# A layernorm, attention and GeGLU kernel on one core: score maxima, fills and splits moved in the prologue and first FFN sections

## The chip, the core and the metric

The kernel runs on one core of a Trainium2 chip. A core has TensorE (matrix products into PSUM, with a separate path that loads weights), VectorE (DVE), ScalarE (ACT) and GpSimd (POOL), which read and write SBUF and PSUM, and SyncE (SP), whose queue here issues the transfers. Each engine works through its own list of instructions in order; one engine waits for another only where an instruction needs its result or its buffer. The metric is the device time of one execution in microseconds (us), taken as the median over runs.

## The reference

x has 2048 rows of 576. The layernorm of x feeds an attention with 32 heads of width 18 and a GeGLU network with 4608 hidden columns, and the two results are joined:

```python
xn = _layernorm(x)
qkv = (xn @ wqkv).reshape(B, S, 3, H, Dh).transpose(2, 0, 3, 1, 4)
q, k, v = qkv[0], qkv[1], qkv[2]
p = _softmax(einsum("bhqd,bhkd->bhqk", q, k) * Dh ** -0.5)
s = einsum("bhqk,bhkd->bhqd", p, v).transpose(0, 2, 1, 3).reshape(B, S, D) @ wo
g = _silu((_gelu(xn @ w_gate) * (xn @ w_up)) @ w_down)
out = x + s * g
```

All values are fp32.

## The kernel before

**Products in parts.** A matrix product is made from operands that are split into a high part, rounded to TensorE's fp32r format, and a low part, what the rounding left. Three products (high by high, high by low, low by high) add up in PSUM. So every weight tile and every activation needs a split ahead of its use: a copy that makes the high part and a subtraction that makes the low one. `split` (L117, L119) does both on GpSimd. `split_ap` (L123, L124) copies on ScalarE and subtracts on GpSimd, and `split_av` copies on ScalarE and subtracts on VectorE.

**Prologue.** Rows come in four blocks of 512. `norm` normalises a block (for block 0 partly on ScalarE), `transposes` turns it on TensorE into five pieces of 128 columns, and `split_t` splits these: the first four into `xth` and `xtl` (L204 for the high part), the last, of 64 columns, into `xtr` (L208). Then `project` multiplies nine weight tiles of 128 query or key columns, in the order (4, 5, 0, 1, 6, 7, 8, 2, 3), with 14 products of 128x512 each (L196); `po` is their sum in PSUM, in three buffers, and `qh` and `ql` are a tile's high and low parts. Weight tiles arrive in `rawp`. The columns that do not fill a tile are the "rest". Tile 4 is the first one and has its own code: its high part is made by ScalarE (`first_hi`), its low part by GpSimd (L355), both at fixed places in their engines' lists. Tiles 5, 0, 1 and so on go through `split_qk`, whose place in GpSimd's list the scheduler chooses. Queries, keys and values are stored to DRAM.

**FFN sections.** The gate and up products are made in sections, each of 27 pairs of 64-row products (L431: `pg` and `pu` are the sums, `xd` the activations, `wh` and `wl` the weights' parts) over 128 hidden columns for 512 rows. A section's pairs take its weights' three groups one after the other, and each group's low part `wl` comes behind its high part. While section n runs, the weights of section n+1 are split: two groups near its start, one at its end. Then `activate` computes the hidden values: a square on ScalarE, VectorE's products at L441 and L445, a tanh on ScalarE at L446, and VectorE's last product at L448. The hidden values are split into `ah` (L457) and `al` (L460).

**Down products.** After every two sections the hidden values meet w_down. `T` holds the two parts of a piece of w_down, which arrives in `rawd` (one buffer). For the first five parts, `down_plain` (L529) makes 48 products `py`, and VectorE adds the sums to `M` (L531). For these, `cut_plain_b` splits w_down: ScalarE copies 128x1152 (L457), GpSimd subtracts (L460), as a hook at pair 4 of the odd section. From the sixth part on, sums of pieces of w_down are made first, by GpSimd into `tsum` (`sums_b`, L494), in the section before they are used, and seven combined products take the place of eight (`down`, L542).

**The lead.** Attention's softmax needs each row's maximum before its exponentials. A score pair for the maxima (`max_pair`: products `pm` at L814, then VectorE's reduction at L815) is issued one unit ahead of the score pair that is used (`pe`, L861, then ScalarE's exponential at L862). So the maxima of the first unit and a quarter of the second, 32 + 8 = 40, must be made before the attention starts with section 11. They are spread over sections 0 to 10; `FIRST` (L41) says how many go into each, and `spread` sets them between the 27 pairs. `KA` and `QT` hold the keys and queries for these products; rows that no load fills are set once to a constant (L761, L764). When 32 maxima of unit 0 are issued, `max_parts(0)` follows: VectorE reduces them to negated maxima `nm` (L821), splits those (L825, L826) and transposes them (L831), SP stores the result and loads it into `QT`. The last three are hooks at numbered pairs of the next section.

**What sets the order.** TensorE's order is the program's. So is SP's from the attention's set-up on. VectorE, ScalarE and GpSimd are ordered by a scheduler, which keeps the items passed to `keep_in_program_order` in their order. The PSUM sums `pgu`, `pm`, `pe`, `acc` and `py` share a ring of three buffers, so a late reduction holds up TensorE's next product.

Of the kernel before, what the change touches and what calls it, by code (L numbers as in the profile page):

```python
# [20 lines left out]
NB = S // TB  # L21
# [19 lines left out]
FIRST = (0, 0, 3, 5, 3, 5, 3, 6, 4, 6, 5)  # L41
# [47 lines left out]
def kernel(ctx: ExitStack, tc: tile.TileContext, x, wqkv, wo, w_gate, w_up, w_down, out):  # L89
# [78 lines left out]

    TERMS = [(0, k, 0) for k in range(KT)] + [(1, k, 0) for k in range(KT)] + [(0, k, 1) for k in range(KT)] \
# [5 lines left out]
    with tc.tile_pool(name="pro", bufs=1) as pro, tc.tile_pool(name="pps", bufs=1, space=PSUM) as pps:  # L175
# [43 lines left out]
        def norm(xr, b, between=None, behind=None):  # L219
            keep = tc.keep_in_program_order if b == 1 else lambda i: i  # L220
            st = pro.tile([P, 4, 8], F32, name="st", bufs=2)
            for j in range(4):
                bs = pro.tile([P, 2, 6], F32, name="bs", bufs=2)
                for h in range(2):
                    one = nc.vector.bn_stats(bs[:, h, :], xr[j][:, 288 * h:288 * h + 288])
                    keep(one)
                if behind and j == 0:
                    behind(one)
                nc.vector.bn_aggr(st[:, j, 0:2], bs)
# [21 lines left out]
            if between:  # L251
                between()
# [95 lines left out]
        def first_hi():  # L348
            tc.keep_in_program_order(nc.scalar.activation(qhi, ahead_qk[0][1], AF.Copy))

        xr = load_x(0)
        last = norm(xr, 0, first_hi, first_loads)
        raw, (raw_r, rest) = ahead_qk.pop(0)[1], ahead_qk.pop(1)
        QR.extend(rest)
        lo = nc.gpsimd.tensor_tensor(qlo, raw, f(qhi), op=ALU.subtract)  # L355
        after(lo, last, "VectorE alone on the first x")
        tc.keep_in_program_order(lo)
        split(QR[0][:, c0], QR[1][:, c0], raw_r[:, c0], tc.keep_in_program_order)
# [4 lines left out]
        for b in range(NB):  # L363
            for n, t in enumerate(ORDER):
                if b == 0 and n == 1:
                    nc.sync.dma_start(zeros.rearrange("i x -> (i x)").rearrange("(p x) -> p x", p=P), zz)
                if n == (2 if b == 0 else 0) and b + 1 < NB:
                    xr = load_x(b + 1)
                if b == 0 and ahead_qk:
                    first = split_qk(*ahead_qk.pop(0))  # L370
                    if n < 3:
                        after(first, last, "VectorE alone on the first x")
                    if n + 4 < NQT:
                        ahead_qk.append(load_qk(ORDER[n + 4]))
                if b == 0 and n == 4:
                    raw_r, VR = load_rest(2 * D, D)
                    split_av(VR[0], VR[1], raw_r, tc.keep_in_program_order)
                if b == 0 and n in (5, 6):
                    raw_v.append(load_wv(n - 5))
                if b == 0 and n in (7, 8):  # L380
                    split_wv(n - 7, raw_v[n - 7])
                project(b, t, xt)
                if n == 4 and b + 1 < NB:
                    norm(xr, b + 1)
# [193 lines left out]
    def section(specials=(), tag="f", slots=False):  # L578
# [20 lines left out]
        if n == 0:  # L599
            load_rawd(0)  # L600
        if g == 0 and (b, r) in FORMED:
            raw = FF["rawd"]
            hook(12, lambda: sums_b(raw))
# [30 lines left out]
    def finish():  # L634
# [16 lines left out]
        if b == 0 and r < PLAIN:  # L651
            if g == 0:
# [101 lines left out]
    with tc.tile_pool(name="att", bufs=1, reuse_waits="tile") as att:  # L754
# [4 lines left out]
        for i, kk in enumerate(KS):  # L759
            for r in range(2):  # L760
                (nc.vector, nc.gpsimd)[i % 2].memset(f(kk[r]), 1.0)  # L761
        QT = [att.tile([P, 2, TB], F32R, name=f"QT{i}") for i in range(3)]
        for t in QT:
            nc.gpsimd.memset(f(t), 0.0)  # L764
# [52 lines left out]
        def max_neg(u):  # L817
# [6 lines left out]
            eng = nc.gpsimd if u > 0 else nc.vector  # L824
            keep(eng.tensor_copy(m2[:, :, 0], n2))  # L825
            keep(eng.tensor_tensor(m2[:, :, 1], n2, f(m2)[:, :, 0], op=SUB))  # L826
# [13 lines left out]
        def max_parts(u):  # L840
            max_neg(u)
            for i, part in ((8, max_turn), (9, max_store), (18, max_end)) if u > 0 else ((0, max_turn), (1, max_store), (14, max_end)):
# [373 lines left out]
```

## Time and profile before

| | |
|---|---|
| time, median of 3 runs | 2559.25 us (2558.43 to 2561.18) |
| profiled execution, its own time | 2558.65 us |
| its span in the trace | 2556.6 us |
| TensorE busy | 2540.1 us (99% of the span) |
| VectorE busy | 2089.0 us (82%) |
| GpSimd busy | 1644.7 us (64%) |
| ScalarE busy | 1462.6 us (57%) |
| mean clock granted to TensorE | 0.999 of full speed |

Rows that are quoted below come from different views of one trace. In the timeline of an engine a row is a start, a busy time, engine, line, operation, output<-inputs, shape, and xN for N instructions in a row; a bracket at its end is the time for which the engine had stood idle, and what ended that. In the list of groups an SPq row is SP's issue of a transfer. Chain rows give a start, a length, engine, name and line. A table of stretches gives a window, its length, and each engine's busy time with the number of instructions.

### The profile page before, as it was taken

What the parts mean: (1) busy time and instruction counts of PE and PEld (TensorE: products, weight loads), DVE (VectorE), ACT (ScalarE), POOL (GpSimd) and SP (SyncE); (2) the same over time, 40 slices, a digit from 0 to 9 for tenths busy, and PEclk for the clock granted to TensorE, in tenths of its full rate; (3) what the DMA queues carried; (4) which work ended last, traced back from release to release, by engine and by line L of the source; (5) the groups of instructions that cost most, each with busy time, mean ns of one, the idle gap of its engine ahead of it and who ended that gap; (6) DMA issues with size and microseconds to landing.
All of it is one profiled execution on the core that took longest, in us unless ns stands there. A gap on an engine that the chain in (4) does not pass through costs nothing.

```text
span 2556.6 us, 52908 instructions
## 1 busy us (share of the span) xinstructions
PE 2540.1 (99%) x20548; PEld 1840.8 (72%) x20548; DVE 2089.0 (82%) x2364; ACT 1462.6 (57%) x1765; POOL 1644.7 (64%) x1714
## 2 busy tenths in 40 slices
PE   9999999999999999999999999999999999999999
PEld 8888866676667766666666666766666776666788
DVE  5326888989888888888887889889898888888367
ACT  3224366666666665566666556555566665556631
POOL 3105588888888875666667566666667666666773
PEclk9999999999999999999999999999999999999999
DMA  8854455555585565677787677666668666665775
GB/s 259 273 187 134 106 165 160 167 168 158 162 220 162 167 172 142 163 169 169 169 194 192 162 169 168 174 168 157 160 159 213 164 173 172 163 167 153 190 212 209
DMA packets 410321, 446.88 MB, mean 175 GB/s; under 512 B 107092, under 2 KB 287060, under 8 KB 410072
## 3 DMA queue, kind: packets, MB, share of 16 engines
q1 hardware_dynamic: 410072, 443.50, 65.4%
q8 instruction: 164, 2.69, 0.5%
q14 instruction: 85, 0.70, 0.1%
HBM read 347.30 MB, written 96.08 MB: 173 GB/s over the span
## 4 chain that ended last, share of the span: by engine, by line
PE 97%; DVE 1%; POOL 1%; ACT 0%; DMA 0%; issue 0%; SPq 0%; POOLq 0%; DVEq 0%; ACTq 0%
PE pg L431 25%; PE acc L878 18%; PE py L542 15%; PE pm L814 9%; PE pe L861 9%; PE pu L431 9%; PE po L196 7%; PE po L1032 2%; PE pgu L431 1%; PE py L529 1%; DVE mx L815 0%; PE pt L268 0%; DMA rawp<-in_A_wqkv_dram 0%; POOL wl L124 0%; ACT pT L862 0%
## 5 line engine op out<-in xcount | busy, mean ns | idle before, releaser
L862 ACT ACTIVATE pT<-pe 128x1024 f32<-128x1024 f32 x1024 | 1048.1, 1027 | 572.7 <-PE pe L861 539.6
L815 DVE TENSOR_REDUCE mx<-pm 128x2 f32<-128x1024 f32 x1024 | 1220.2, 1224 | 166.5 <-PE pm L814 150.5
L431 PE MATMUL pu<-xd,wh 64*128 64x512 f32 x2466 | 902.2, 396 | 0.0
L431 PE MATMUL pg<-xd,wh 64*128 64x512 f32 x2466 | 901.3, 396 | 0.0
L431 PEld LDWEIGHTS pg<-xd,wh 64*128 64x128 f32 x2466 | 455.0, 185 | 114.4 <-issue 55.6
L431 PE MATMUL pg<-xd,wl 64*128 64x512 f32 x1233 | 481.4, 390 | 1.1 <-POOL wl L124 1.1
L431 PE MATMUL pu<-xd,wl 64*128 64x512 f32 x1233 | 481.6, 391 | 0.0
L431 PEld LDWEIGHTS pu<-xd,wh 64*128 64x128 f32 x2466 | 455.0, 184 | 17.5 <-ACT xd L160 0.2
L878 PE MATMUL acc<-pT,VS 128*32 128x512 f32 x4096 | 466.0, 595 | 0.0
L117 POOL TENSOR_SCALAR wh<-raw 128x384 fp32r<-128x384 f32 x402 | 218.7, 546 | 372.9 <-PE pu L431 262.0
L119 POOL TENSOR_TENSOR wl<-raw,wh 128x384 fp32r<-128x384 f32 x402 | 415.8, 1036 | 28.5
L814 PE MATMUL pm<-KA,QT 64*128 64x512 f32 x2048 | 413.7, 395 | 6.4 <-ACT pT L862 3.3
L861 PE MATMUL pe<-QT,KA 64*128 64x512 f32 x2048 | 411.0, 392 | 0.0
L542 PE MATMUL py<-T,ah 128*128 128x288 f32 x1876 | 380.6, 298 | 0.0
L549 DVE TENSOR_TENSOR M<-py,M 128x576 f32<-128x576 f32 x448 | 339.6, 758 | 31.7 <-PE py L542 18.1
L542 PEld LDWEIGHTS py<-T,ah 128*128 128x128 f32 x1876 | 298.4, 188 | 54.0 <-issue 54.0
L460 POOL TENSOR_TENSOR al<-h,ah 128x512 fp32r<-128x512 f32 (+1 forms) x143 | 295.6, 2067 | 61.5 <-ACT ah L457 51.7
L878 PEld LDWEIGHTS acc<-pT,VS 128*32 128x32 f32 x4096 | 120.1, 109 | 276.8 <-issue 229.7
L542 PE MATMUL py<-T,al 128*128 128x288 f32 x938 | 275.7, 294 | 0.0
L861 PEld LDWEIGHTS pe<-QT,KA 64*128 64x128 f32 x2048 | 192.9, 184 | 109.7 <-DVE mx L815 24.4
L431 PEld LDWEIGHTS pg<-xd,wl 64*128 64x128 f32 x1233 | 227.6, 185 | 36.4 <-POOL wl L124 2.0
L814 PEld LDWEIGHTS pm<-KA,QT 64*128 64x128 f32 x2048 | 198.9, 185 | 54.6 <-ACT pT L862 9.3
(174 smaller groups left out, 3001.7 us busy)
## 6 DMA issues: line engine op xcount, KB each, us to landing
T<-ts SPq DMA_DIRECT2D x98, 576.0 KB
KA<-qk SPq DMA_DIRECT2D x768, 72.0 KB
T<-ts SPq DMA_DIRECT2D x98, 432.0 KB
raw<-in_B_w_gate_dram SPq DMA_DIRECT2D x144, 288.0 KB
raw<-in_B_w_up_dram SPq DMA_DIRECT2D x144, 288.0 KB
ts<-T SPq DMA_DIRECT2D x36, 576.0 KB
VS<-vs SPq DMA_DIRECT2D x128, 152.0 KB
qk<-t SPq DMA_DIRECT2D x72, 256.0 KB
```

The source lines that it names most:

```text
L117: first = nc.gpsimd.tensor_scalar(hi, raw, 1.0, 1.0, op0=ALU.mult, op1=ALU.mult)
L119: keep(nc.gpsimd.tensor_tensor(lo, raw, f(hi), op=ALU.subtract))
L196: nc.tensor.matmul(o, st, m, start=(i == 0), stop=(i == len(terms) - 1))
L431: nc.tensor.matmul(o, w[1 + wp][k][rr, c, :], xd[k][xp][rr, c, :], start=(i == 0), stop=(i == len(terms) - 1))
L460: keep(two.tensor_tensor(lo, raw, f(hi), op=ALU.subtract))
L542: nc.tensor.matmul(py[:, t, 0:DC], h[:, i, tt], T[:, w, k], start=n == 0, stop=n == 2)
L549: nc.vector.tensor_tensor(M[:, m], py[:, :, 0:DC], M[:, m], op=ALU.add)
L814: nc.tensor.matmul(pm[:, a], QS[u, r][rr, t * P:(t + 1) * P], KS[(u * NA + c) % KB][r][rr, :], start=True, stop=True)
L815: nc.vector.tensor_reduce(MX[u][:, 2 * r:2 * r + 2, t, c], pm, axis=AX.X, op=ALU.max)
L861: nc.tensor.matmul(pe[:, a], KS[(u * NA + c) % KB][r][rr, t * P:(t + 1) * P], QS[u, r][rr, :], start=True, stop=True)
L862: nc.scalar.activation(PT[u, kt][:, 2 * r:2 * r + 2, :], pe, AF.Exp, scale=SCALE)
L878: nc.tensor.matmul(ACC[u][32 * a:32 * a + 32, :], VS[(u * NA + c) % VB][:, v:v + 32], pt[:, a, :], start=first, stop=last, skip_group_chec ...
```

## The change

1. **Maxima.** `FIRST` is another table with the same total of 40. The 32nd maximum is now issued in section 8, where it was in section 9, so `max_parts(0)` runs a section sooner, and so does one load of keys that depends on the same count. Its three hooks stand at pairs 8, 9 and 18, where they stood at 0, 1 and 14, and the split of the negated maxima is on GpSimd, where it was on VectorE.
2. **Fills.** All of `KA` and `QT` is filled by VectorE; before, GpSimd filled six of the fourteen `KA` rows and the three `QT` tiles.
3. **First w_down piece.** Its split is a hook at the last pair of section 0; it was at pair 4 of section 1.
4. **Tanh table.** An activation with Tanh on the constant `eps` stands at the start of block 3's projection, so that ScalarE loads its table there.
5. **First key tile.** Both parts of tile 4 are split on GpSimd, in program order, and `first_hi` is gone. The rest's split follows, and a new helper, `behind`, keeps the splits of the next tiles after the rest's first operation. It sets an order on GpSimd and adds no wait on a semaphore.

```diff
-FIRST = (0, 0, 3, 5, 3, 5, 3, 6, 4, 6, 5)
+FIRST = (0, 0, 4, 5, 4, 5, 4, 5, 5, 4, 4)
...
+    def behind(what, before):
+        tc.add_manual_dep(what.ins, before.ins.name, mybir.DependencyInfo(
+            mybir.DependencyClass.NoSync, mybir.DependencyReason.DATA), reason="issue order")
...
-        def first_hi():
-            tc.keep_in_program_order(nc.scalar.activation(qhi, ahead_qk[0][1], AF.Copy))
-
         xr = load_x(0)
-        last = norm(xr, 0, first_hi, first_loads)
+        last = norm(xr, 0, True, first_loads)
         raw, (raw_r, rest) = ahead_qk.pop(0)[1], ahead_qk.pop(1)
         QR.extend(rest)
-        lo = nc.gpsimd.tensor_tensor(qlo, raw, f(qhi), op=ALU.subtract)
-        after(lo, last, "VectorE alone on the first x")
-        tc.keep_in_program_order(lo)
-        split(QR[0][:, c0], QR[1][:, c0], raw_r[:, c0], tc.keep_in_program_order)
+        after(split(qhi, qlo, raw, tc.keep_in_program_order), last, "VectorE alone on the first x")
+        lo = split(QR[0][:, c0], QR[1][:, c0], raw_r[:, c0], tc.keep_in_program_order)
...
         for b in range(NB):
+            if b == NB - 1:
+                tc.keep_in_program_order(nc.scalar.activation(eps, eps, AF.Tanh))
...
                     if n < 3:
                         after(first, last, "VectorE alone on the first x")
+                        behind(first, lo)
...
         if n == 0:
             load_rawd(0)
+            hook(len(pairs) - 1, lambda: cut_plain_b(FF["rawd"]))
...
-            if g == 0:
+            if g == 0 and r > 0:
                 raw = FF["rawd"]
                 hook(4, lambda: cut_plain_b(raw))
...
-        for i, kk in enumerate(KS):
+        for kk in KS:
             for r in range(2):
-                (nc.vector, nc.gpsimd)[i % 2].memset(f(kk[r]), 1.0)
+                nc.vector.memset(f(kk[r]), 1.0)
         QT = [att.tile([P, 2, TB], F32R, name=f"QT{i}") for i in range(3)]
         for t in QT:
-            nc.gpsimd.memset(f(t), 0.0)
+            nc.vector.memset(f(t), 0.0)
...
-            eng = nc.gpsimd if u > 0 else nc.vector
-            keep(eng.tensor_copy(m2[:, :, 0], n2))
-            keep(eng.tensor_tensor(m2[:, :, 1], n2, f(m2)[:, :, 0], op=SUB))
+            keep(nc.gpsimd.tensor_copy(m2[:, :, 0], n2))
+            keep(nc.gpsimd.tensor_tensor(m2[:, :, 1], n2, f(m2)[:, :, 0], op=SUB))
...
-            for i, part in ((8, max_turn), (9, max_store), (18, max_end)) if u > 0 else ((0, max_turn), (1, max_store), (14, max_end)):
+            for i, part in ((8, max_turn), (9, max_store), (18, max_end)):
```

GpSimd's list at the program's start, before: `qh_120` and `ql_121` are tile 4's parts (the first is not here, ScalarE makes it), `qh_264` and `ql_265` tile 5's, `rest_0` the rest's.

```order
L248 COPY xx<-xx 128x64 x2
L117 TENSOR_SCALAR qh_264<-rawp 128x512
L119 TENSOR_TENSOR ql_265<-rawp,qh_264 128x512
L355 TENSOR_TENSOR ql_121<-rawp,qh_120 128x512
L117 TENSOR_SCALAR rest_0_141<-raw 128x128
L117 TENSOR_SCALAR qh_292<-rawp 128x512
L119 TENSOR_TENSOR rest_0_142<-raw,rest_0_141 128x128
```

The same place in the changed kernel:

```order
L252 COPY xx<-xx 128x64 x2
L117 TENSOR_SCALAR qh_120<-rawp 128x512
L119 TENSOR_TENSOR ql_121<-rawp,qh_120 128x512
L117 TENSOR_SCALAR rest_0_141<-raw 128x128
L117 TENSOR_SCALAR qh_264<-rawp 128x512
L119 TENSOR_TENSOR rest_0_142<-raw,rest_0_141 128x128
L119 TENSOR_TENSOR ql_265<-rawp,qh_264 128x512
```

Tile 4's high part has come to GpSimd, and both parts stand ahead of tile 5; the rest's first operation has moved ahead of tile 5 as well.

GpSimd's list at the first FFN sections, before. `wl` is a weight group's low part, `T<-rawd` the split of w_down, `al` the low part of a section's hidden values.

```order
L124 TENSOR_TENSOR wl<-raw,wh 128x384 x2
L761 MEMSET KA 128x512 x6
L764 MEMSET QT_1947 128x1024
L764 MEMSET QT_1948 128x1024
L764 MEMSET QT_1949 128x1024
L124 TENSOR_TENSOR wl<-raw,wh 128x384
L460 TENSOR_TENSOR al<-h_2031,ah 128x512
L124 TENSOR_TENSOR wl<-raw,wh 128x384 x2
L460 TENSOR_TENSOR T<-rawd,T 128x1152
L124 TENSOR_TENSOR wl<-raw,wh 128x384
L460 TENSOR_TENSOR al<-h_2127,ah 128x512
```

And changed:

```order
L124 TENSOR_TENSOR wl<-raw,wh 128x384 x2
L460 TENSOR_TENSOR T<-rawd,T 128x1152
L124 TENSOR_TENSOR wl<-raw,wh 128x384
L460 TENSOR_TENSOR al<-h_2034,ah 128x512
L124 TENSOR_TENSOR wl<-raw,wh 128x384 x3
L460 TENSOR_TENSOR al<-h_2128,ah 128x512
L124 TENSOR_TENSOR wl<-raw,wh 128x384 x3
```

The fills are gone, and the w_down split stands ahead of section 1's last weight group and section 0's `al`, where it stood behind them and two groups of section 2.

VectorE's list at the end of the lead, before: from the last down products of sections 6 and 7 (L531) to section 10's reductions and hidden values.

```order
L531 TENSOR_TENSOR M<-M,py 128x576 x5
L815 TENSOR_REDUCE mx<-pm 128x2 x6
L441 SCALAR_TENSOR_TENSOR h_3193<-h_3193,pgu 128x512
L445 TENSOR_TENSOR t_3196<-t_3196,pgu 128x512
L448 SCALAR_TENSOR_TENSOR h_3193<-h_3193,t_3196 128x512
L821 TENSOR_REDUCE nm<-mx 128x16
L825 CAST m_3203<-nm 128x2x8
L826 TENSOR_TENSOR m_3203<-nm,m_3203 128x2x8
L831 STREAM_TRANSPOSE mt<-m_3203 128x32
L815 TENSOR_REDUCE mx<-pm 128x2 x5
L441 SCALAR_TENSOR_TENSOR h_3320<-h_3320,pg 128x512
```

And changed (the lines behind the new code are one higher); the rows run from section 7's reductions to section 9's:

```order
L816 TENSOR_REDUCE mx<-pm 128x2 x5
L441 SCALAR_TENSOR_TENSOR h_2932<-h_2932,pgu 128x512
L445 TENSOR_TENSOR t_2935<-t_2935,pgu 128x512
L448 SCALAR_TENSOR_TENSOR h_2932<-h_2932,t_2935 128x512
L816 TENSOR_REDUCE mx<-pm 128x2 x5
L441 SCALAR_TENSOR_TENSOR h_3041<-h_3041,pg 128x512
L445 TENSOR_TENSOR t_3044<-t_3044,pg 128x512
L531 TENSOR_TENSOR M<-M,py 128x576
L448 SCALAR_TENSOR_TENSOR h_3041<-h_3041,t_3044 128x512
L822 TENSOR_REDUCE nm<-mx 128x16
L531 TENSOR_TENSOR M<-M,py 128x576 x5
L831 STREAM_TRANSPOSE mt<-m_3051 128x32
L816 TENSOR_REDUCE mx<-pm 128x2 x4
```

The sequence for `nm` to `mt` has left its place between section 9's hidden values and section 10's reductions, and is a section earlier, around the down products; L825 and L826 are no longer on VectorE.

More of the change, by code (lines that the diff above doesn't have):

```diff
@@ L217, in load_x, with norm @@
             return xr
-        def norm(xr, b, between=None, behind=None):
+        def norm(xr, b, between=False, on_first=None):
             keep = tc.keep_in_program_order if b == 1 else lambda i: i
@@ L226, in norm @@
                     keep(one)
-                if behind and j == 0:
-                    behind(one)
+                if on_first and j == 0:
+                    on_first(one)
                 nc.vector.bn_aggr(st[:, j, 0:2], bs)
@@ L250, in norm @@
                     act(*ends, AF.Copy)
-            if between:
-                between()
             return last
```

## Prediction

> **What bounds the kernel now.** I read the page first (which engine is full), then a table of stretches that I cut where the stages end, then the list of what TensorE waited for, then the instructions around each of its gaps.
>
> ```profile
> 0.00:14.41 14.41, 11.23 (x68) 9.98 (x69) 9.62 (x31) 6.54 (x12) 6.39 (x23) 1.00 0.81 215
> 14.41:197.98 183.57, 183.57 (x1011) 160.29 (x1011) 68.92 (x132) 48.68 (x105) 27.66 (x28) 1.00 0.73 237
> 197.98:219.38 21.40, 20.25 (x170) 16.01 (x169) 6.96 (x8) 11.33 (x21) 18.91 (x21) 1.00 0.58 166
> 283.94:310.88 26.94, 24.07 (x179) 19.39 (x179) 23.79 (x28) 7.06 (x12) 19.44 (x19) 0.94 0.38 93
> 325.00:2400.00 2075.00, 2072.30 (x17312) 1437.72 (x17310) 1814.34 (x1960) 1307.34 (x1495) 1443.16 (x1513) 1.00 0.66 169
> 2400.00:2556.60 156.60, 150.86 (x1194) 130.81 (x1190) 98.84 (x130) 48.15 (x68) 88.68 (x81) 1.00 0.70 215
> sum 2556.60, PE 2540.10 PEld 1840.76 DVE 2088.98 ACT 1462.58 POOL 1644.66; mean PE 317.51 PEld 230.09 DVE 261.12 ACT 182.82 POOL 205.58
> ```
>
> Columns: stretch, its length, then busy time of PE, weight loads, DVE, ACT and POOL, the granted clock, the share of the DMA engines, GB/s. TensorE is busy for 2540.1 of 2556.6 us, so 16.5 us are all that scheduling can win, and 8.4 of them (2.70 in the long middle and 5.74 at the end) lie in stretches the change does not touch. What it touches is the start (3.18 us idle), the first three FFN sections (1.15) and the stretch from 283.94 (2.87, and the only one below full clock). The prize is some 8 us of 2559, 0.3%.
>
> **Part 1, the first key weight tile.** The split of tile 4 moves from ACT (high part) and POOL (low part, behind tile 5's whole split) to POOL alone, ahead of tile 5.
>
> ```profile
> 12.70 0.98 PE L196 MATMUL po<-xth,qh 128*128 128x512 f32 x2 [0.25 <-ACT xth L204]
> 14.41 0.50 PE L196 MATMUL po<-xth,ql 128*128 128x512 f32 x1 [0.72 <-POOL ql L355]
> 17.31 0.86 PE L196 MATMUL po<-xth,qh 128*128 128x512 f32 x3
> 11.15 0.62 POOL L117 TENSOR_SCALAR qh<-rawp 128x512 fp32r<-128x512 f32 x1 [0.51 <-DMA rawp<-in_A_wqkv_dram]
> 11.85 1.27 POOL L119 TENSOR_TENSOR ql<-rawp,qh 128x512 fp32r<-128x512 f32 x1
> 13.08 1.28 POOL L355 TENSOR_TENSOR ql<-rawp,qh 128x512 fp32r<-128x512 f32 x1
> 12.05 2.06 ACT L204 ACTIVATE xth<-pt 128x512 fp32r<-128x512 f32 x4
> 15.20 0.69 DVE L208 TENSOR_TENSOR xtr<-pt,xtr 64x512 fp32r<-64x512 f32 x1
> ```
>
> TensorE waits for the low part until 14.36. With tile 4 first, POOL does 0.62 and 1.27 from 11.15 at the latest, and the low part is there by 13.1, 1.3 us sooner. Not all of that counts: xth comes one piece per half microsecond until 14.1, and the last two products need xtr, which VectorE ends at 15.89 in either kernel. Two products of 0.23 us after that (TensorE's own pace: 17.31 minus 14.41 over 12 products) end the tile at 16.4 instead of 17.31. **Gain 0.9 us**, between 0 (POOL starts later than I think) and 1.3. It should last, since the following 183.57 us show no idle TensorE. Taking the high part from ACT gives nothing by itself, because xth waits for the transposes.
>
> **Part 2, fills, tanh table and first w_down split.**
>
> ```profile
> 188.74 4.27 DVE L761 MEMSET KA<- 128x512 f32 x8
> 200.91 2.87 POOL L761 MEMSET KA<- 128x512 f32 x6
> 203.71 2.75 POOL L764 MEMSET QT<- 128x1024 f32 x3
> 198.94 0.39 SPq L576 DMA_DIRECT2D rawd<-in_B_w_down_dram  x1
> 205.53 1.28 ACT L446 ACT_TABLE_LOAD   x1
> 209.59 1.15 ACT L457 ACTIVATE T<-rawd 128x1152 fp32r<-128x1152 f32 x1
> 212.12 2.68 POOL L460 TENSOR_TENSOR T<-rawd,T 128x1152 fp32r<-128x1152 f32 x1
> 207.50 0.69 DVE L448 SCALAR_TENSOR_TENSOR h<-h,t 128x512 f32<-128x512 f32 x1 [1.15 <-ACT h L446]
> 213.81 1.54 DVE L448 SCALAR_TENSOR_TENSOR h<-h,t 128x512 f32<-128x512 f32 x1
> 210.35 0.39 PE L431 MATMUL pu<-xd,wh 64*128 64x512 f32 x1
> 211.24 0.50 PE L431 MATMUL pg<-xd,wl 64*128 64x512 f32 x1 [0.50 <-POOL wl L124]
> 216.26 0.50 PE L431 MATMUL pg<-xd,wl 64*128 64x512 f32 x1 [0.64 <-POOL wl L124]
> 233.55 0.39 PE L431 MATMUL pg<-xd,wh 64*128 64x512 f32 x1
> 219.38 6.57 PE py L529 x48
> 240.56 6.57 PE py L529 x48
> ```
>
> Section 2 waits twice for low weights from a POOL that is 18.91 of 21.40 us busy. Its length is 219.38 minus 210.35, 9.03 us; section 4, with the same three maxima, takes 240.56 minus 233.55, 7.01. So 2.0 us are to be had. POOL loses the fills, 2.87 + 2.75 us. On VectorE they take 6 x 0.53 (4.27 over 8) and, the QT tiles being twice as long, 3 x 1.07, together 6.4; VectorE is idle for 14.44 of the 21.40 us from 197.98, so they cost nothing. POOL also does the 2.68 us split before section 1's last low weights instead of among section 2's. ACT's table load of 1.28 us goes to the start of the last projection, where ACT's share is 48.68 of 183.57 and three product buffers cover it: cost nothing, and it brings the first tanh, the activation's split and the weights behind them forward by that much.
>
> The new order has its own wait: the split waits on ACT for the w_down transfer, issued at 198.94. If that takes about 4.5 us (estimate from the next fence's 296.61 to 301.63, an upper bound), ACT ends it by 204.6 and POOL by 207.3; the last low weights of section 1 follow at 208.3, and TensorE wants them at about 208.5 (sections 0 and 1 take 6.2 us each from 197.98, and these are 19 pairs in). Section 2's first low weights come at 210.7 to 211.3, against 210.6 wanted; the later value if VectorE's gate product at 207 meets POOL's split, as at 213.81 (1.54 us beside it, 0.69 alone). Of the 2.0 us, 0.1 to 0.7 remain; I take 0.4. **Gain 1.6 us**, between 0.6 (transfer a microsecond later) and 2.0. The page SBUF — State Buffer of the Trainium skill (SBUF: two separate sides) says that VectorE with two SBUF inputs and GpSimd lock each other out for a whole instruction; by it the product would wait only for the split's end at 207.3, and this term would be 1.7. The 1.54 us agrees with a lockout.
>
> **Part 3, the maxima.** Sections 2 to 10 issued 3, 5, 3, 5, 3, 6, 4, 6, 5 and now 4, 5, 4, 5, 4, 5, 5, 4, 4.
>
> ```profile
> 230.33 0.23 PE pm L814 x2
> 261.76 6.57 PE py L529 x48
> 283.94 6.57 PE py L529 x48
> 310.88 6.58 PE py L529 x48
> 307.07 0.79 PE L814 MATMUL pm<-KA,QT 64*128 64x512 f32 x2 [2.87 <-DVE mx L815]
> 309.00:310.00 1.00, 1.00 (x8) 0.80 (x6) 1.00 (x2) 0.00 (x0) 0.98 (x1) 0.50 0.06 12
> 296.61 0.39 SPq L576 DMA_DIRECT2D rawd<-in_B_w_down_dram  x1
> 301.63 1.44 POOL L494 TENSOR_TENSOR tsum<-rawd 128x576 f32<-128x576 f32 x1 [0.92 <-DMA rawd<-in_B_w_down_dram]
> 305.59 1.26 POOL L460 TENSOR_TENSOR al<-h,ah 128x512 fp32r<-128x512 f32 x1
> ```
>
> The down products (py) start every two sections, so their distances are the pair's cost: 21.18 us with 8 maxima, 21.20 with 8, 22.18 with 10, 26.94 with 11. One maximum costs TensorE 0.23, so 11 should cost 21.9. The 5 us beyond are VectorE: six reductions in section 9, then the first block's negated maxima and their transpose in front of section 10's reductions; TensorE stops for 2.87 us and then runs at half clock. Now the pairs have 9, 9, 10, 8: 21.41, 21.41, 21.64, 21.18, together 85.64 against 91.50. Section 2 gets one more, 0.23. That is 5.6 us less.
>
> The maxima's end moves a section ahead, beside the down products of sections 6 and 7, and its two small copies from VectorE to POOL, under 0.5 us in a POOL that idles there. What is late next: TensorE comes to the last down products at 283.94 + 21.18 = 305.1 on this trace's clock, and needs the low part of section 9's activation about 0.7 us in (five products of 0.137). POOL makes it only at 306.85, behind three sums that wait for w_down, and nothing in the change moves that; in addition SP now issues the four maxima stores, two reloads and a value load ahead of that w_down load, up to 0.6 us. New stall 1.0 to 1.7, I take 1.5. **Gain 4.1 us**, up to 5.6 if POOL is sooner, down to 2.4 if the stall grows to 1.5 plus 1.7 of slow clock (3.4 us at half). Between stalls of 0.64 us, which left the clock at 1.00, and 2.87, which halved it, no row says where the limit is.
>
> The page TensorE: Matmul & The Clock Gate of the Trainium skill (Why this matters for your kernels) allows idle gaps up to about 3 us; the trace differs, since 2.87 us were enough. By the page even a stall of 2.5 us is safe, and the halved clock among the rivals would pass its chance to the forecast.
>
> **Sum.** 0.9 + 1.6 + 4.1 = 6.6 us off the profiled execution's 2558.65 (span 2556.6 and 2.05 around it) is 2552.05; the median of the runs, 2559.25, lies 0.6 above that execution, so I predict **2552.6**.
>
> **Rivals.**
> - *POOL keeps up.* No stall at the last down products: 8.1 us gained, 2551.1. For it: VectorE's product at 302 no longer slows POOL's sums. Against: the sums start when w_down lands, which is not sooner.
> - *The new stall halves the clock.* Stall 2.5 us and 1.7 of slow clock: gain 3.9, 2555.3, within the noise of the measurement. For it: the extra DMAs ahead of w_down. Against: the stall must pass some 2.5 us.
> - *Slower: the first w_down transfer is late.* ACT now holds section 0's activation and section 1's weights behind it. Every microsecond that it lands after about 203.6 is one of TensorE idle, and past 2.5 us the clock halves for 1.7 more. To eat 6.6 us it must land at 208.5, 9.6 after its issue; the bound from the trace is 5. At 209.5 the time is 2560.5 or above.
> - *No effect.* The lead's end is also held by something else, such as the score's first exponentials behind the w_down copies on ACT, and what is gained is waited for there: about 2558. Against: the windows after 325 show TensorE full, and that wait hangs on the down products themselves, which come sooner too.
>
> **How the numbers follow.** A measurement tells this kernel from no change at about 0.2%, 5.1 us, so faster means under 2554.1. Forecast 0.62 (0.06 of it above that line, when the low ends of two parts meet), POOL keeps up 0.12, halved clock 0.15, no effect 0.05, slower 0.06. Faster 0.68, same 0.26, slower 0.06. The parts' ends add to gains of 3.0 and 8.9, 2556.3 and 2550.4; with the runs' own scatter the range is 2549.5 to 2556.5.
>
> **What the new profile would show.** Right: the second tile's first product at about 16.4; no wait for low weights in section 2, or one under 0.7; down products at even distances of 21.2 to 21.7; no wait for the reductions and a clock of 1.00 there; one new wait of TensorE on POOL's low activation at the last down products. Wrong: ACT idle for w_down ahead of its first copy, a clock below 1 anywhere before 325, or a gap at the start of the scores longer than the present 0.9.

## The result and the profile after

The changed kernel takes 2553.07 us (median of 8 runs, 2552.49 to 2554.42). The kernel before, run eight times beside it, takes 2559.63. The ratio is 0.9973, with a 95% interval of 0.9964 to 0.9982: 6.6 us or 0.27% less, where 2552.6 us was forecast.

The stretches of the changed kernel that answer to two of those shown of before (columns as there): the first three sections, and from the fourth of the lead's down products to the fifth:

```profile
197.40:217.46 20.06, 20.06 (x172) 15.79 (x171) 8.65 (x13) 9.89 (x19) 13.27 (x11) 1.00 0.68 163
282.01:303.05 21.04, 21.04 (x174) 17.99 (x172) 18.20 (x24) 7.11 (x12) 14.12 (x15) 1.00 0.47 104
```

In the first three sections TensorE stands idle no more (it did for 1.15 us), and GpSimd is busy for 13.27 us where it was for 18.91. In the second stretch the clock is 1.00 where it was 0.94, and TensorE is not idle at all, where it was for 2.87 us. Right behind it there is a new idle time of 1.33 us. What ended it is in the list of TensorE's waits, and who was late stands in the timelines of TensorE, GpSimd, ScalarE and SP's queue:

```profile
PE py L529 <- POOL al L460: 1.3, 1, 1.3
```

```profile
16.73 1.09 PE L200 MATMUL po<-xth,qh 128*128 128x512 f32 x4
282.01 0.53 PE L529 MATMUL py<-T,ah 128*128 128x288 f32 x2
303.05 0.53 PE L529 MATMUL py<-T,ah 128*128 128x288 f32 x2
305.31 0.40 PE L529 MATMUL py<-T,al 128*128 128x288 f32 x1 [1.33 <-POOL al L460]
10.76 0.62 POOL L117 TENSOR_SCALAR qh<-rawp 128x512 fp32r<-128x512 f32 x1
203.90 2.69 POOL L460 TENSOR_TENSOR T<-rawd,T 128x1152 fp32r<-128x1152 f32 x1 [3.51 <-PE pg L431]
300.45 1.43 POOL L494 TENSOR_TENSOR tsum<-rawd 128x576 f32<-128x576 f32 x1 [1.53 <-DMA rawd<-in_B_w_down_dram]
303.98 1.27 POOL L460 TENSOR_TENSOR al<-h,ah 128x512 fp32r<-128x512 f32 x1
202.66 1.17 ACT L457 ACTIVATE T<-rawd 128x1152 fp32r<-128x1152 f32 x1 [3.91 <-DMA rawd<-in_B_w_down_dram]
299.59 0.63 ACT L457 ACTIVATE ah<-h 128x512 fp32r<-128x512 f32 x1 [1.03 <-DVE h L448]
294.83 0.55 SPq L849 DMA_DIRECT2D QT<-mxT  x2
295.91 0.46 SPq L576 DMA_DIRECT2D rawd<-in_B_w_down_dram  x1
```

The new wait is the one that was forecast. Five products of the last down group run; the sixth needs the low activation. Its high part is ready at 300.22, but GpSimd has the three sums of w_down ahead of it and waits for their transfer until 300.45.

Two marks tell where the time went: the lead's down products, and the first combined down products behind the lead (`py` of L542), from the chain. Of the changed kernel, and behind it the last mark of before:

```profile
217.46 6.57 PE py L529 x48
238.96 6.57 PE py L529 x48
260.38 6.57 PE py L529 x48
339.92 5.74 PE py L542 x42
```

```profile
346.04 5.74 PE py L542 x42
```

The changed kernel is 0.58 us ahead at the second key tile (17.31 against 16.73), 1.92 at the first down products (219.38 against 217.46) and 6.12 behind the lead. Behind that the two kernels have the same program. This profiled execution, the slowest of the eight (2554.42, where the prediction's sum gave 2552.05 for it), loses 2 us of the lead again on its way to the end; its span is 4.1 us shorter. From the first combined products to the end of the span before takes 2210.6 us and this execution 2212.6; in all the traces of this case but that of `gaps`, which has other code there, it is 2210.5 to 2213.4. So a loss of 2 us is within what executions of this part differ by, and only the medians, which are 6.6 apart, can be held against the forecast.

### The profile page after: what moved, and what is told of

It is laid out like the page before. It is cut to its first block, busy times and chain, and to the rows that moved or that the text cites. A ratio compares the mean times of both kernels' runs of the same rounds, so it can differ in the third digit from the quotient of the medians.

```text
span 2552.5 us, 52902 instructions
## 1 busy us (share of the span) xinstructions
PE 2539.3 (99%) x20548; PEld 1840.7 (72%) x20548; DVE 2088.0 (82%) x2371; ACT 1462.3 (57%) x1765; POOL 1640.4 (64%) x1708
## 4 chain that ended last, share of the span: by engine, by line
PE 97%; DMA 1%; DVE 1%; POOL 1%; ACT 0%; issue 0%; SPq 0%; DVEq 0%; POOLq 0%; ACTq 0%
PE pg L431 24%; PE acc L878 18%; PE py L542 15%; PE pu L431 10%; PE pm L815 9%; PE pe L861 9%; PE po L200 7%; PE po L1032 2%; PE pgu L431 1%; PE py L529 1%; DMA xd<-xhs 0%; PE pt L270 0%; POOL wl L124 0%; DMA raw<-in_B_w_up_dram 0%; DMA xx<-in_A_x_dram 0%
## 5 line engine op out<-in xcount | busy, mean ns | idle before, releaser
L542 PE MATMUL py<-T,ah 128*128 128x288 f32 x1876 | 380.8, 298 | 0.0
L542 PEld LDWEIGHTS py<-T,ah 128*128 128x128 f32 x1876 | 298.6, 188 | 54.0 <-issue 54.0
L542 PE MATMUL py<-T,al 128*128 128x288 f32 x938 | 275.8, 294 | 0.0
L431 PEld LDWEIGHTS pu<-xd,wl 64*128 64x128 f32 x1233 | 227.2, 184 | 11.2
```

The costliest lines, as they stand in the source:

```text
L431: nc.tensor.matmul(o, w[1 + wp][k][rr, c, :], xd[k][xp][rr, c, :], start=(i == 0), stop=(i == len(terms) - 1))
L542: nc.tensor.matmul(py[:, t, 0:DC], h[:, i, tt], T[:, w, k], start=n == 0, stop=n == 2)
```

## The experiments

Two distances are used throughout: from the first product of the second key tile to the first down products ("to the down products"), and to the first combined ones ("to the combined"). They leave out the start of the program, where x lands at a slightly different time in every execution. Before: 202.07 and 328.73. Changed: 200.73 and 323.19.

### Each part alone

`p1` is the kernel before with the first tile's edit, `p2` with the fills, the w_down split and the tanh table, `p3` with the table of maxima, their sooner end and its copies on GpSimd:

```diff
p1
+        after(split(qhi, qlo, raw, tc.keep_in_program_order), last, "VectorE alone on the first x")
+        lo = split(QR[0][:, c0], QR[1][:, c0], raw_r[:, c0], tc.keep_in_program_order)
...
+                        behind(first, lo)
p2
+                tc.keep_in_program_order(nc.scalar.activation(eps, eps, AF.Tanh))
...
+            hook(len(pairs) - 1, lambda: cut_plain_b(FF["rawd"]))
...
+            nc.vector.memset(f(t), 0.0)
p3
+FIRST = (0, 0, 4, 5, 4, 5, 4, 5, 5, 4, 4)
...
+            keep(nc.gpsimd.tensor_copy(m2[:, :, 0], n2))
...
+            for i, part in ((8, max_turn), (9, max_store), (18, max_end)):
```

> The kernel before with part 1 alone (first key tile split on GpSimd ahead of the second). Parts add up: the second tile's first product starts at 16.7 us instead of 17.31, the lead's first down products at 218.8 instead of 219.38, and the first combined down products at 345.4 instead of 346.04, so 0.6 us are kept to the lead's end. Rival, what is gained early is waited for later: 16.7 as well, but 219.4 or 346.0.

> The kernel before with part 2 alone (fills on VectorE, first w_down split a section sooner, tanh table in the last projection). Parts add up: no wait for low weights in section 2, the first down products at 217.8 instead of 219.38 (1.57 sooner), the first combined ones at 344.5 instead of 346.04. Rival, part 2 works only on top of part 1's 0.6 us: low weights still late by 0.5, first down products at 218.8 or later.

> The kernel before with part 3 alone (the new table of maxima, the maxima's end a section sooner and its copies on GpSimd). Parts add up: down products at distances of 21.4 to 21.7 but the last, with one stall of 1.3 us on GpSimd's low activation and no drop of the clock; first combined down products at 342.1 instead of 346.04. Rival, most of the gain needs parts 1 and 2: 344 or later.

| | second tile | to the down products | to the combined | one run |
|---|---|---|---|---|
| before | 17.31 | 202.07 | 328.73 | 2558.65 |
| p1 | 16.49 | 202.05 | 328.16 | 2558.90 |
| p2 | 16.27 | 200.48 | 325.49 | 2555.92 |
| p3 | 16.77 | 201.76 | 323.03 | 2553.07 |
| changed | 16.73 | 200.73 | 323.19 | 2554.42 |

p1 keeps what it wins, as was expected. p2 wins 1.59 us to the down products, the 1.57 expected, and more after them: its stall on the reductions is 2.40 us long instead of 2.87, and the clock stays up behind it (the windows are shown below). p3 got 1.8 us more than was expected (342.1 less 17.31 is 324.8): its distance to the combined is that of the whole change. So the parts do not add up. With the new table in, part 2's one microsecond (201.76 against 200.73) is gone again by the end of the lead. The timelines of GpSimd and TensorE in p3 show where:

```profile
300.00 1.84 POOL L494 TENSOR_TENSOR tsum<-rawd 128x576 f32<-128x576 f32 x1
303.96 1.27 POOL L460 TENSOR_TENSOR al<-h,ah 128x512 fp32r<-128x512 f32 x1
305.29 0.40 PE L529 MATMUL py<-T,al 128*128 128x288 f32 x1 [0.32 <-POOL al L460]
```

The low activation is begun at 303.96 here and at 303.98 in the changed kernel, though TensorE gets there a microsecond sooner in the latter (303.05 against 304.04; the second tiles start at 16.73 and 16.77); p3's TensorE waits 0.3 us for it, the changed kernel's 1.3.

### Why the low activation is late

`al_first` puts it ahead of the sums, with `behind` (GpSimd's order alone); `reload_late` leaves it and moves the reload of the maxima behind the w_down load in SP's order; `p3_rounds` is p3 again, timed.

```diff
al_first
...
+        FF["al"] = cut(ah[:, 2 * g:2 * g + 2], al[:, 2 * g:2 * g + 2], h[:, 0:2], nc.scalar, nc.gpsimd)
...
-        keep(nc.gpsimd.tensor_tensor(t[:, 1:3], q[:, 0:4:2], q[:, 1:4:2], op=ALU.add))
+        one = nc.gpsimd.tensor_tensor(t[:, 1:3], q[:, 0:4:2], q[:, 1:4:2], op=ALU.add)
+        keep(one)
+        if "al" in FF:
+            behind(one, FF.pop("al"))
reload_late
-            for i, part in ((8, max_turn), (9, max_store), (18, max_end)):
+            def end_next(u):
+                FF["hooks"].setdefault(2, []).append(lambda: max_end(u))
+
+            for i, part in ((8, max_turn), (9, max_store), (18, max_end if u > 0 else end_next)):
```

> The changed kernel with GpSimd's order altered at one place: section 9's low activation ahead of the three sums that wait for w_down. If the new stall comes from that order, TensorE's 1.3 us at the last down products go to 0 to 0.2, and the first combined down products start at 338.6 instead of 339.92; time about 2551.8. Rival, the next thing is just as late (VectorE's sums of the down products, or GpSimd's next weights, now 1.3 us behind): another wait of about 1 us close by, 339.6 or later, 2553.

> The changed kernel with the reload of the maxima behind the w_down load in SP's order instead of ahead of it. If SP's order holds up w_down (the load was issued at 295.91 us, 1.1 after its buffer was free), it goes out at 294.9, GpSimd's sums start at 299.3 instead of 300.45, TensorE's stall at the last down products falls from 1.3 to 0.4 or less, and the first combined down products start 1.0 sooner after the second tile than in the changed kernel (322.2 instead of 323.2 us behind it). Rival, the transfer lands no sooner because others share the engines, or the scores wait for the reload instead: no gain, 323.2 or later.

> The kernel before with part 3 alone, timed in rounds. The first look showed the low activation ready at 305.2 us in this kernel and in the changed one, since both wait for the same w_down transfer. If so, what parts 1 and 2 win is waited away there, and this kernel takes as long as the changed one: median 2553.0, within 0.5. Rival, the parts add up and the first look was a lucky execution: 1.8 us more than the changed kernel, 2554.9.

GpSimd's rows of al_first (its L496 is the first sum, L494 elsewhere), then SP's and GpSimd's of reload_late (its L852 is the reload):

```profile
300.36 1.29 POOL L460 TENSOR_TENSOR al<-h,ah 128x512 fp32r<-128x512 f32 x1 [1.36 <-ACT ah L457]
301.61 1.44 POOL L496 TENSOR_TENSOR tsum<-rawd 128x576 f32<-128x576 f32 x1
```

```profile
294.60 0.39 SPq L576 DMA_DIRECT2D rawd<-in_B_w_down_dram  x1
297.05 0.97 SPq L852 DMA_DIRECT2D QT<-mxT  x2
298.67 1.97 POOL L494 TENSOR_TENSOR tsum<-rawd 128x576 f32<-128x576 f32 x1
302.74 1.29 POOL L460 TENSOR_TENSOR al<-h,ah 128x512 fp32r<-128x512 f32 x1
```

In al_first the stall is gone. It is 321.92 us to the combined, 1.27 less than in the changed kernel (1.3 expected), with a new wait of 0.3 for low weights. Its median is 2552.25 (6 runs, ratio 0.9970, 0.9958 to 0.9982): the best version by its trace and by its median, but its interval and the changed kernel's overlap almost wholly, so the times alone don't show it faster. In reload_late the w_down load goes out at 294.60 instead of 295.91, the stall is 0.3, and it is 322.30 to the combined (322.2 expected). Its median is 2552.66 (10 runs, ratio 0.9976, 0.9967 to 0.9985). Both causes hold: SP's order delays the transfer, and GpSimd's order hands the delay on. What SP waited for from 286 to 300 us tells why the microsecond is lost; the first row is of the changed kernel, the other two of p3:

```profile
SPq L849 <- DMA mxT<-mt: 2.9, 2, 2.4
SPq L848 <- DMA mxT<-mt: 1.0, 2, 0.6
SPq L576 <- POOL T L460: 0.8, 1, 0.8
```

In p3 the w_down load goes out (295.80) when its buffer is free, that is when GpSimd's split of the piece before ends (295.78). In the changed kernel that split ends at 294.78, but the reload ahead of the load waits for the store of the maxima to land, 2.9 us instead of 1.0, and the load goes out at 295.91. Why the store lands later there is not shown.

p3_rounds has a median of 2552.84 (11 runs), within the 0.5 that was expected. But the kernel before took 2558.11 beside it, so the ratio is 0.9980 (0.9971 to 0.9989), 5.3 us rather than 6.6. The two intervals overlap; the times leave open whether part 3 alone is worth eight tenths of the change or all of it. The traces are firmer: 323.03 and 323.19 to the combined in p3's two profiles, 323.19 in the changed kernel. Of what p3 lacks, that leaves part 1, at the program's start.

### The first tile, in thirteen executions

Every profile taken gives part 1 another sample. From the first transpose to the second tile's first product, the six kernels with the new order need 6.67 or 6.68 us each (changed, p1, al_first, reload_late, `late` and `gaps` below). Seven with the old order need 6.86 to 9.59: p2 6.86, p3 6.87, flat 6.87, before 7.41, split 7.69, tanh 7.70 and fills 9.59 (the last four kernels follow below). In p3_rounds the clock fell during the transposes, so it is left out. The difference is TensorE's wait for tile 4's low part, 0.18 to 1.35 us, and behind it is tile 5's transfer, which stood ahead in GpSimd's list. Of `fills`:

```profile
11.66 0.62 POOL L117 TENSOR_SCALAR qh<-rawp 128x512 fp32r<-128x512 f32 x1 [1.14 <-DMA rawp<-in_A_wqkv_dram]
14.93 0.78 PE L196 MATMUL po<-xth,ql 128*128 128x512 f32 x1 [1.35 <-POOL ql L355]
```

So part 1 is worth 0.2 us where that transfer is in time, 0.7 to 1.0 where it is late, and 2.9 in the execution where the clock fell as well (0.63 instead of 0.40 for a product of the same kind at 15.51).

### Inside part 2

One edit each on the kernel before: the fills, the tanh table, the split.

```diff
fills
-                (nc.vector, nc.gpsimd)[i % 2].memset(f(kk[r]), 1.0)
+                nc.vector.memset(f(kk[r]), 1.0)
...
-            nc.gpsimd.memset(f(t), 0.0)
+            nc.vector.memset(f(t), 0.0)
tanh
+                tc.keep_in_program_order(nc.scalar.activation(eps, eps, AF.Tanh))
split
+            hook(len(pairs) - 1, lambda: cut_plain_b(FF["rawd"]))
...
-            if g == 0:
+            if g == 0 and r > 0:
```

> The kernel before with the fills on VectorE alone. The distance from the second tile's first product to the first down products is 202.07 us before and 200.48 with part 2. If the low activation (which waits for ScalarE until 208.9) is what holds GpSimd up, both waits for low weights stay: 201.8 to 202.1. Rival, GpSimd's 5.6 us of fills are what is late: 200.5 to 200.9.

> The kernel before with the tanh table loaded in the last projection alone. If ScalarE's 1.28 us stand in the chain that ends in section 2's low weights, the first wait for them goes and the second shrinks to 0.2 or less: distance from the second tile to the first down products 200.8 to 201.1 instead of 202.07. Rival, the load is covered before and after: 202.0.

> The kernel before with the first w_down split a section sooner alone. GpSimd ends the fills at 206.5, then the split at 209.1, then section 1's last low weights at 210.1, about 1.5 us after TensorE wants them: a new wait in section 1, and section 2's waits gone; distance to the first down products 202.4 instead of 202.07. Rival, the split's place alone makes the gain: 200.5 to 201.

To the down products: fills 202.09, tanh 201.86, split 202.35, against 202.07 before and 200.48 with all three. Alone they give nothing, 0.2 and a loss of 0.3; together 1.6. Fills and split came as expected, tanh did not. Its tanh begins at 206.08 instead of 206.83, though the second tile began 0.30 later. But VectorE's last product (L450 is L448 in this kernel) now meets GpSimd's low weights (206.72, 1.02 us) and takes 1.54 us instead of 0.69:

```profile
206.72 1.02 POOL L124 TENSOR_TENSOR wl<-raw,wh 128x384 fp32r<-128x384 f32 x1
206.75 1.54 DVE L450 SCALAR_TENSOR_TENSOR h<-h,t 128x512 f32<-128x512 f32 x1
```

In p2, where the fills are away too, the same product begins at 205.68 and takes 0.99 us. This fits edits that need each other; it is not shown further, since no run has two of the three. The page SBUF — State Buffer of the Trainium skill (SBUF: two separate sides) has the two engines lock each other out in such a pair; the trace agrees: the product ends at 208.29, 0.55 after GpSimd's operation. For split, the row of its new wait in section 1, as worked out (1.5 expected):

```profile
210.73 0.50 PE L431 MATMUL pgu<-xd,wl 64*128 64x512 f32 x2 [1.85 <-POOL wl L124]
```

### Inside part 3

`flat` spreads the maxima but leaves their end behind section 9's reductions, on VectorE:

```diff
-FIRST = (0, 0, 3, 5, 3, 5, 3, 6, 4, 6, 5)
+FIRST = (0, 0, 4, 4, 4, 4, 4, 5, 5, 5, 5)
```

> The kernel before with the maxima spread evenly (4, 4, 4, 4, 4, 5, 5, 5, 5 in sections 2 to 10) but their end still in section 10 and on VectorE. If it is VectorE's backlog of six reductions that counts, the stall on the reductions falls to about 1.7 us, the clock stays up, and the first combined down products start 325.3 us after the second tile instead of 328.7. Rival, the sooner end of the maxima is what counts: a stall of 2.5 or more, 327 to 328.5.

```profile
300.84 1.14 DVE L825 CAST m<-nm 128x16 fp32r<-128x16 f32 x1
304.13 0.50 PE L814 MATMUL pm<-KA,QT 64*128 64x512 f32 x2 [2.90 <-DVE mx L815]
```

The rival wins: the stall is 2.90 us, as long as before, the clock falls, and it is 327.11 us to the combined. With one reduction less, TensorE comes sooner as well, and waits for the same thing: the sequence from the negated maxima (300.60) to their transpose (302.97) on VectorE, ahead of section 10's reductions. Spreading alone gives 1.6 us, the sooner end with its copies on GpSimd and its own table the other 4.1 (327.11 against 323.03), the clock's fall among them. No run parts the sooner end from the copies.

### The slower rival, made to happen

`late` issues the first w_down load behind the first keys and queries:

```diff
+            load_k(0)
+            load_q(0)
             load_rawd(0)
...
-            if n == 0:
-                load_k(0)
-                load_q(0)
```

> The changed kernel with the first w_down load behind the first key and query loads in SP's order, so that it is issued at about 205.7 us instead of 198.4 and lands at about 210. The slower rival of the prediction, put to the test: ScalarE's copy and all behind it wait, TensorE loses 6.4 us of idle time and 1.7 of slow clock, first down products 8 us later than in the changed kernel, time 2561. The other way, other buffers cover a part: 3 us or less, 2556.

```profile
209.07 1.16 ACT L457 ACTIVATE T<-rawd 128x1152 fp32r<-128x1152 f32 x1 [1.93 <-DMA rawd<-in_B_w_down_dram]
210.70 0.50 PE L431 MATMUL pgu<-xd,wh 64*128 64x512 f32 x2 [2.96 <-ACT wh L123]
213.94 0.79 PE L431 MATMUL pgu<-xd,wl 64*128 64x512 f32 x2 [2.74 <-POOL wl L124]
```

The load goes out at 204.59 and lands at 209.0, 6.4 us later than in the changed kernel (202.6). TensorE stands idle for 2.96 and 2.74 us, and slow clock makes the rest (two windows at half speed, from 211.87 to 218.70, with 4.76 us of work in them): 8.0 us more to the down products (208.76), the 8 that were expected, and one run of 2560.04. By the prediction's own rule (idle for every microsecond after 203.6, and 1.7 of clock) a landing at 209.0 costs 7.1, so the rival's price was right to 0.9. In the changed kernel the transfer is 4.3 us on its way, and the rival has no case.

### From which idle time the clock falls

In `gaps` GpSimd repeats the low activation of every second section, three times and up to three fifths of a fourth, so that TensorE has to wait for it:

```diff
+            if ATT.start + 1 < FF["n"] < ATT.stop:
+                for w in (5, 5, 5, FF["n"] // G % 4):
+                    if w:
+                        keep(two.tensor_tensor(al[:, 2:2 + w], h[:, 1:1 + w], f(ah[:, 2:2 + w]), op=ALU.subtract))
```

> The changed kernel with GpSimd writing the low activation of each second section three times more, and 0 to 3 fifths of it a fourth time, from the attention's start on: about 9 us more against some 7.6 us of slack, so TensorE should stand idle for 1 to 4 us at many down products. It shows from which idle time the clock drops. If the chip judges fixed windows of 3.41 us, as the one drop of 306.83 to 310.24 looks, gaps under about 1.7 us never halve the clock, gaps of 2 to 3 do so in some cases and not in others, and longer ones always. Rival, a limit on the gap's own length (2.5, as the prediction put it): every gap above it halves the clock and none below.

Its list of waits has 62 of these, the longest of 5.4 us:

```profile
PE py L546 <- POOL al L482: 157.2, 62, 5.4
```

The clock record of every trace here has its changes on a grid of 3.413 us (in before, half clock lasts 3.413 and the full clock behind it 2245.97, which is 658 times that), whose place in the program differs from one execution to the next. Cutting gaps into the windows of its grid gives 823. Two of them with their successors (length, then TensorE's busy time; the granted clock is the last column but two):

```profile
1251.39:1254.80 3.41, 1.67 (x13) 1.44 (x12) 1.47 (x2) 0.00 (x0) 3.25 (x4) 1.00 0.44 111
1254.80:1258.21 3.41, 3.41 (x16) 3.41 (x16) 1.91 (x3) 0.00 (x0) 3.24 (x5) 0.50 0.54 135
1558.59:1562.00 3.41, 1.76 (x13) 1.53 (x12) 1.43 (x3) 0.00 (x0) 3.25 (x4) 1.00 0.52 144
1562.00:1565.41 3.41, 3.41 (x28) 3.16 (x28) 3.24 (x5) 0.00 (x0) 3.24 (x5) 1.00 0.65 147
```

In `gaps` a window in which TensorE was busy for less than about half halves the clock of the next: all 44 full-clock windows followed by a slow one had at most 1.74 us of work, all 719 others at least 1.74. A slow window needs more to end it: 16 with up to 2.77 us were followed by another, 44 with 2.89 or more were not. The first expectation was right and the rival, a limit on the gap's length, is out. In the lead the two kinds stand side by side. p1 lost the clock after an idle time of 2.15 us and before after 2.87; split, whose idle time of 2.98 was cut in two by a window's edge, kept it, and p2 kept it after one of 2.40. First before, then p1, split and p2:

```profile
303.42:306.83 3.41, 0.78 (x8) 0.31 (x4) 3.31 (x6) 0.63 (x1) 3.41 (x4) 1.00 0.02 5
306.83:310.24 3.41, 3.17 (x16) 2.48 (x18) 3.41 (x4) 0.00 (x0) 2.98 (x5) 0.50 0.06 10
```

```profile
302.17:305.58 3.41, 1.26 (x14) 0.71 (x10) 3.31 (x7) 0.63 (x1) 3.33 (x4) 1.00 0.01 1
305.58:308.99 3.41, 3.41 (x16) 2.76 (x18) 3.41 (x4) 0.00 (x0) 2.63 (x4) 0.50 0.08 19
```

```profile
302.76:306.17 3.41, 1.92 (x18) 1.25 (x14) 3.34 (x4) 0.63 (x1) 3.41 (x3) 1.00 0.14 24
306.17:309.58 3.41, 1.92 (x14) 1.35 (x16) 3.38 (x5) 0.00 (x0) 3.25 (x5) 1.00 0.04 5
```

```profile
299.97:303.38 3.41, 1.63 (x16) 1.00 (x12) 3.31 (x5) 0.60 (x1) 3.41 (x4) 1.00 0.08 12
303.38:306.80 3.42, 2.81 (x20) 1.85 (x21) 3.42 (x4) 0.21 (x1) 3.25 (x5) 1.00 0.04 7
```

p2's window has less work than the 1.74 us of `gaps` and the clock still stays up. At the program's start it is the other way round: a window of `fills` with 1.81 us of work loses the clock.

```profile
11.56:14.98 3.42, 1.81 (x11) 0.97 (x8) 2.41 (x4) 3.42 (x8) 3.24 (x4) 1.00 0.72 174
14.98:18.39 3.41, 3.41 (x8) 2.73 (x9) 3.33 (x4) 0.54 (x2) 3.41 (x5) 0.50 0.73 199
```

So the windows are shown, but the limit in them is known only to lie about the middle, from 1.6 to 1.8 us of the work that the profile counts.

## Why the prediction was right

The forecast was a gain of 6.6 us and the medians give 6.6; the waits that went are the ones named, and the new wait is at its place. That the sum met the number so closely is in part luck, since two errors in it cancel (part 3 below). The parts, by the marks:

| part | forecast | measured in the two profiles | what the runs add |
|---|---|---|---|
| 1, first tile | 0.9 | 0.58 at the second tile, 0.74 from the first transpose | 0.2 to 2.9, by when tile 5's transfer lands |
| 2, first sections | 1.6 | 1.57 (1.34 to the down products, and 0.23 for one maximum more) | 1.59 alone; gone again by the end of the lead |
| 3, maxima, net of the new stall | 4.1 | 3.97 (6.12 less the other two) | 5.7 alone, all that the change has behind the second tile |
| new stall within it | 1.5 | 1.33 | 0.3 without parts 1 and 2 |

- **Part 1** was sized from one execution, and its cause was put as GpSimd's order. That is a part of it: the order costs 0.2 us, and the rest is what a late transfer of the second tile adds, which the trace of before showed in a bracket (0.51, rawp) that the working did not use. The second tile starts at 16.73 where 16.4 was worked out, because x came 0.16 us later in this execution and the two products behind `xtr` began 0.15 after it was ready.
- **Part 2** kept 0.4 us of wait for section 2's low weights; there was none. w_down was there at 202.66, 0.8 us before the 203.4 that the bound gave, and GpSimd ended its split at 206.6 where 207.3 was worked out. That the three edits win next to nothing one by one was not said: the working took their costs one by one, as savings of the same engine.
- **Part 3** rested on distances of down products of 21.41, 21.41, 21.64 and 21.18; they are 21.50 (238.96 less 217.46), 21.42, 21.63 and 21.04 up to the stalled group at 303.05. The stall was read from the right row, but the working held its time fixed: the low activation at 306.85, which nothing in the change was to move. In p3 it is ready at 305.23, on the clock of before 305.8 (the second tiles start at 16.77 and 17.31), 1.1 us sooner, and part 3's own stall is 0.3 us, not 1.5. In the changed kernel it is ready at 305.25, no sooner than in p3, though TensorE comes a microsecond sooner: GpSimd's low activation is set by the w_down transfer, so what part 2 wins ahead of it is waited away. So part 3 alone was forecast 1.6 us too small (4.1 for 5.7, of which 1.2 are the stall), and the 1.6 of part 2 do not last behind it. The two errors cancel in the sum, which is luck. Of the two causes that it named for the stall of 2.87, the reductions hardly count (flat), the maxima's end does.
- **Rivals.** *POOL keeps up* did not happen; al_first shows its price, 1.3 us. *The new stall halves the clock* could not: an idle time of 1.33 us leaves every window at least 2.1 of its 3.4 us busy. The limit of 2.5 us on which its 0.15 stood was no limit. *Slower* was priced 0.9 us under what `late` lost: its rule gives 5.4 us of idle time where 5.7 were measured, and one window at half speed where there were two, 2.4 us and not 1.7. (By the same rule a landing at 209.5 makes 2560.2, not the 2560.5 that stands there.)
- **Signs.** One of the signs of being wrong did show: ScalarE stands idle for 3.91 us ahead of its first copy of w_down, until 202.66. It cost TensorE nothing, for in before ScalarE stood idle there as well, for TensorE's sums, until 204.43.
- The clock also decided what there was to win. Its fall cost before 1.6 us in the profiled execution (half of the 3.17 us of work in the slow window). By the grid an idle time of 2.87 us keeps the clock only where a window's edge leaves less than about 1.71 us on either side; with windows that lie anywhere with equal chance, that is, as an estimate, 0.55 of 3.41 us (2 x 1.71 - 2.87), so the clock falls in 0.84 of the executions. So a gain read from one trace holds that much of chance; here the median over the runs agreed.

## To carry to other kernels

When a stall is removed, ask which transfer the next waiting engine hangs on: if that engine is held by a load and not by the work that was made shorter, all gains ahead of it run into the same wait, and putting the one operation that TensorE needs ahead of the ones that wait for the load (or that load ahead in its queue) is worth more than a further saving upstream (here 1.3 us, in al_first). Price edits that free one engine together, since any of them alone may only move its work beside another's. A wait that differs from one execution to the next, such as one on a transfer at the program's start, wants several traces before it is put into a sum.

## What was not expected of the hardware

The clock of TensorE changes by fixed windows of 3.413 us: a window with less than about half of TensorE's time busy halves the next one, and a half-speed window has to be busy for some 2.8 us to end it (2.77 us did not, 2.89 did, in `gaps`). The limit is not sharp over the traces here: windows of 1.63 us (p2) kept the clock, and windows of 1.74 (`gaps`) and 1.81 (`fills`) lost it. An idle time of 2.15 us cost the clock in one execution and 2.98 us did not in another. The page TensorE: Matmul & The Clock Gate of the Trainium skill (What's actually happening) has the window, its length and that it runs free; it asks for a whole idle window before the clock falls, and there the runs differ. A single wait under 1.6 us between full work was safe in every trace. The 1.35 us of fills were not: they share their window with a wait of 0.25 us and with the short products of the transposes, and which of these mattered is not shown.
